# A fused attention and mixture-of-experts kernel: earlier q/k loads, spread setup steps, a fixed TensorE order in seven pairs, early first expert rows, and outputs issued behind weight conversions

## The chip, the core and the metric

The kernel runs on one core of a Trainium2 chip. A core has TensorE (called PE in the profile, its weight loads PEld), VectorE (DVE), ScalarE (ACT), GpSimd (POOL) and SyncE (SP, here a queue that issues DMAs). The metric is the device time of one execution in microseconds (us); lower is better.

## What is computed

First, causal attention over 8 batches and 8 heads with 576 positions and 64 channels, with a bias from a running sum of `max(s, 0)`. Its output is then the input of a routed network with 8 experts: each of the 4608 tokens takes the expert with the largest logit.

```python
scores = scale * np.matmul(q, k.transpose(0, 1, 3, 2))
cum = np.cumsum(np.maximum(s, 0.0), axis=-1)
bias = -(cum[:, :, :, None] - cum[:, :, None, :])
scores = np.where(causal, -1000000000.0, scores + np.minimum(bias, 0.0))
attn = softmax(scores)                     # written out in the reference
x = np.matmul(attn, v)                     # to (4608, 512)
logits = x @ w_gate + modality_bias[modality_id]
e_idx = np.argmax(logits, axis=1)
h = np.maximum(x[mask] @ w1[e], 0.0)       # for each expert e, its tokens
out[mask] = gate_w[mask, None] * (h @ w2[e])
```

## The kernel before, in words

**Attention** (`Attn`, lines 42 to 613). The work is cut into 32 *pairs*: one head of two batches. Eight pairs (the heads) make one of four *groups* of batches. A pair has nine score steps, in the order `ORDER = (3, 7, 2, 6, 8, 1, 5, 0, 4)`; the loop `run` (line 556) counts them with one counter `k`, so pair `k // 9`, position `k % 9`, 288 steps in all. A step does `score` (TensorE: a high product on line 374 and a low product on line 396, or lines 409 and 410 for step 8; DVE adds the mask and takes the maximum on line 398; ACT takes the exponential on line 421) and, three steps later (`LAG`), `trans`: TensorE transposes on line 441 into a PSUM tile `pt`, which ACT copies out on line 445. When a pair is through, `whole` multiplies by V (line 528), ACT copies `oT` (line 531), and line 348 projects into `x`, the network's rows. The last pair uses `tail` instead (lines 482 to 507).

q and k are split into a high and a low part for fp32r products: `prep` (line 314) makes them for the next pair on POOL, four high copies on line 324 and four differences on line 328. It needs the raw q and k of that pair (`load_qk`, line 306, issued by SP two pairs ahead, into two buffers each) and must not overwrite the `KA` buffer until the pair that still uses it is through its scores. `place` puts bias rows in by small DMAs (lines 264 and 283, six a pair in pairs 2 to 7; from pair 8 on two, lines 251 and 252, out of tables in DRAM that `save`, lines 189 and 191, writes in steps 21, 30, 39 and 48).

**What sets the order.** Instructions are traced in program order and a compile-time list scheduler orders each engine's queue by priority and by its own estimate of when operands are ready; at run time each queue is strictly in order. `issue_after(i)` adds an edge: what is traced within it comes behind `i` on `i`'s engine. `high_priority(offset)` raises priorities. `STRICT` (line 34) puts the transposes of steps 27 to 71 (pairs 3 to 7) behind the latest TensorE instruction of the attention; scores are free. `newest()` puts setup work behind the newest work of each engine. Setup functions run at given steps (dictionary `setup`, line 1414); a generator in `bg` goes on at every step when it yields `False`, at step n when it yields n.

**Routing** (`Route`). After each group, `group` computes logits, the one-hot expert, positions (ten small matmuls, line 775) and scatters the group's rows to per-expert lists in DRAM (line 799, nine scatters a group, 36 in all). After group 2, `first` builds the table `t2` of the first six blocks from groups 0 to 2 alone, which need the first 27 scatters. `pad` (line 817) writes 256 zero rows behind each of the eight lists. `rest` builds the tables `t3` and `t4`; their rows need all scatters and pads.

**Experts** (`Moe`, line 974). 18 blocks of 256 rows of one expert (6 of `t2`, 12 of `t3`), then a mixed block `two` and a loop for what is left. For a block, SP fetches rows (`gather2`, lines 1106 and 1107, into `xr` and `tg`) and `xt` (line 1113) makes them `xT`: two DVE transposes into PSUM (line 1120), a high copy on ACT (line 1122), a low difference on DVE (line 1123). The block's first half is 96 matmuls (line 1170, `hp`), evacuated as ReLU into high and low parts (lines 1172 and 1173); the second half is 48 matmuls (line 1145, `y`), evacuated with the gate by ACT (line 1155) and DVE (line 1153) into `ys`, which POOL scatters to the output (line 1156). The next block's `xt` is traced in the middle of a block (`mid`).

The weights of a block are eight *chunks* of 512 KB (four of w1, four of w2), loaded by SP (lines 1008 and 1010) into six raw buffers, and split into high (ACT, line 1033) and low (DVE, line 1034) in one of 13 converted buffers: 4 `wca`, 5 `wcb`, 4 `wcc`. Chunks 0 to 3 are converted by POOL (lines 1031 and 1034) while the attention ends (`early`, from step 278); the others come in steps of the blocks. `stop` limits how many chunks block 0 takes. The `wcc` buffers lie where the attention's rows `x` lay (pools `xp0` and `xp1`).

## Time and profile before

| | us |
|---|---|
| three runs | 810.08, 810.64, 811.33 (median 810.64) |
| profiled execution, device time | 811.94 |
| its span, first to last instruction | 810.2 |
| outside the span | 1.74 |
| mean granted TensorE clock | 0.988 |

How to read it: the page and the trace's views give times in us from the span's start. A timeline row is: start, duration, engine, line, operation, output tile <- input tiles, shapes, count, and in brackets the engine's idle time before it with what ended it. A row of the windows view is a stretch, its length, then for each engine the busy time and in brackets the number of instructions, the granted TensorE clock, the share of the 16 DMA engines and GB/s. "SPq" and "POOLq" are the engines' queues. Lines that several operations share are told apart by the tile names.

The attention lies from about 8 to 373 us, the expert blocks from 375 to 788 us, the rest to 810 us.

### The profile page before, as it was taken

To read this page: it belongs to the slowest core of one execution; us is meant where nothing else is said; L and a number is where in the kernel's file an instruction comes from. 1 tells how busy PE (TensorE), PEld (TensorE's weight loads), DVE (VectorE), ACT (ScalarE), POOL (GpSimd) and SP (SyncE) were. 2 spreads that over 40 slices of the span, in tenths; PEclk is the share of its full clock that TensorE was granted. 3 is DMA by queue.
4 is the path that set the end of the run, shared out by engine and by line. 5 is a ranking of instruction groups with operands and counts; after the bars stand their busy time and mean duration, and the time that the engine had idled before them with its cause. 6 is when DMAs were issued, how large, how long until landed. Compare 5 with 4: busy or idle time off the path is not lost. (4 is left out here: it accounts for less than half of the span.)

```text
span 810.2 us, 17263 instructions
## 1 busy us (share of the span) xinstructions
PE 790.2 (98%) x5796; PEld 684.1 (84%) x5796; DVE 565.5 (70%) x1441; ACT 519.6 (64%) x1165; POOL 363.9 (45%) x383
## 2 busy tenths in 40 slices
PE   8999999999999999998999999999999999999996
PEld 7787788888888888887888998888889998988884
DVE  7655667655766667767679786677777776677664
ACT  6877788878788778875455444555555555455553
POOL 8958877898789978993600100110000000001001
PEclk8999999999999999998999999999999999999999
DMA  7376644777567765659997897587878777877740
GB/s 238 116 214 195 220 147 155 258 235 230 158 183 240 229 186 175 213 160 292 300 319 240 282 291 256 174 273 228 255 252 263 249 247 240 261 256 259 257 170 29
DMA packets 88168, 181.21 MB, mean 224 GB/s; under 512 B 13785, under 2 KB 33113, under 8 KB 87950
## 3 DMA queue, kind: packets, MB, share of 16 engines
q1 hardware_dynamic: 82238, 160.03, 63.7%
q0 software_dynamic: 5840, 20.06, 6.3%
q8 instruction: 46, 0.75, 0.4%
q14 instruction: 44, 0.36, 0.1%
HBM read 143.59 MB, written 26.80 MB: 210 GB/s over the span
## 5 line engine op out<-in xcount | busy, mean ns | idle before, releaser
L1156 POOL DMA_INDIRECT out<-ys,oi x36 | 38.3, 1064 | 354.6 <-ACT ys L1155 274.8
L421 ACT ACTIVATE pe<-pe,mx 128x512 f32<-128x512 f32 (+3 forms) x256 | 142.3, 559 | 15.8 <-DVE mx L398 15.7
L398 DVE CUSTOM_DVE_ANT_0 pe<-sp,mk 128x512 f32<-128x512 f32 (+3 forms) x256 | 117.1, 482 | 49.1 <-PE sp L396 24.7
L445 ACT COPY PT<-pt 128x512 f32<-128x512 f32 (+1 forms) x192 | 94.2, 504 | 29.0 <-PE pt L441 28.9
L441 PE MATMUL pt<-ident,pe 128*128 128x128 f32 x640 | 106.4, 279 | 0.9 <-ACT PT L445 0.9
L374 PE MATMUL sp<-KA,QH 128*128 128x256 f32 (+2 forms) x256 | 97.4, 390 | 4.4 <-POOL KA L238 2.4
L1172 ACT ACTIVATE hT<-hp 128x512 fp32r<-128x512 f32 x72 | 43.1, 599 | 88.5 <-PE hp L1170 86.1
L1170 PE MATMUL hp<-xT,wca 128*128 128x256 f32 x624 | 88.6, 286 | 3.9 <-ACT xT L1122 2.5
L1170 PE MATMUL hp<-xT,wcb 128*128 128x256 f32 x648 | 90.1, 282 | 0.2 <-DVE wcb L1034 0.2
L328 POOL TENSOR_TENSOR QL<-rawq,QH 64x576 fp32r<-64x576 f32 x62 | 87.1, 1421 | 0.3
L328 POOL TENSOR_TENSOR KA<-rawk,KA 64x576 fp32r<-64x576 f32 x62 | 86.4, 1412 | 0.1
L1170 PEld LDWEIGHTS hp<-xT,wca 128*128 128x128 f32 x624 | 81.1, 194 | 5.5 <-issue 2.6
L396 PE MATMUL sp<-KB,QL 76*128 76x256 f32 (+2 forms) x256 | 84.5, 336 | 0.2 <-DMA QL<-ek 0.2
L441 PEld LDWEIGHTS pt<-ident,pe 128*128 128x128 f32 x640 | 77.4, 145 | 8.6 <-ACT PT L445 1.7
L528 PE MATMUL o<-PT,V 128*64 128x512 f32 (+1 forms) x496 | 84.5, 440 | 0.0
L1170 PEld LDWEIGHTS hp<-xT,wcb 128*128 128x128 f32 x648 | 83.3, 188 | 1.1 <-DVE wcb L1034 0.4
L1145 PE MATMUL y<-wcb,hT 128*128 128x512 f32 x336 | 80.9, 396 | 0.0
L1173 DVE SCALAR_TENSOR_TENSOR hT<-hp,hT 128x512 fp32r<-128x512 f32 x72 | 49.5, 688 | 42.7 <-ACT hT L1172 42.3
L1145 PEld LDWEIGHTS y<-wcb,hT 128*128 128x128 f32 x336 | 62.6, 188 | 14.5
L528 PEld LDWEIGHTS sp<-PT,V 128*64 128x64 f32 x620 | 38.2, 137 | 33.3 <-issue 28.5
L1170 PE MATMUL hp<-xT,wcc 128*128 128x256 f32 x456 | 64.3, 279 | 1.1 <-DVE hT L1173 0.7
L1145 PE MATMUL y<-wcc,hT 128*128 128x512 f32 x264 | 63.3, 395 | 0.0
(294 smaller groups left out, 1663.0 us busy)
## 6 DMA issues: line engine op xcount, KB each, us to landing
wrbw<-in_w SPq DMA_DIRECT2D x104, 512.0 KB
wraw<-in_w SPq DMA_DIRECT2D x56, 512.0 KB
rawq<-in_qkv SPq DMA_DIRECT2D x31, 576.0 KB
rawk<-in_qkv SPq DMA_DIRECT2D x31, 576.0 KB
V<-in_qkv SPq DMA_DIRECT2D x32, 320.0 KB
xr<-lists SPq DMA_DIRECT2D x72, 128.0 KB
KB<-KA SPq DMA_DIRECT2D x62, 144.0 KB
lists<-z SPq DMA_DIRECT2D x8, 576.0 KB
```

The lines of the kernel that those rows point to most:

```text
L328: self.last = nc.gpsimd.tensor_tensor(o, i, h, ALU.subtract).ins
L374: self.pe.append(self.nc.tensor.matmul(sp[:, :nn], QH[:, q0:q0 + P], self.KA[u][:, ab, :nn], start=True, stop=False).ins)
L396: self.pe.append(nc.tensor.matmul(sp[:, :nn], QL[:EXT, q0:q0 + P], KB[:EXT, ab, :nn], start=False, stop=True).ins)
L398: ins = nc.vector.tensor_tensor_reduce(out=t[:, :n], in0=sp[:, :n], in1=self.mk[:, 512 - n:512], scale=-0.125, scalar=3.0e38, op0=ALU.add, ...
L421: self.act = nc.scalar.activation(t[:, :n], t[:, :n], AF.Exp, bias=m, scale=-1.0, accum_out=st["sums"][:, o:o + 1]).ins
L441: self.pe.append(nc.tensor.transpose(out=pt[:, o:o + P], in_=pe[:, P * j:P * j + P], identity=self.ident).ins)
L445: return cp(w[:, :, :, v:v + P], pt[:, :n * (1 + both)].rearrange("p (a j q) -> p a j q", a=1 + both, q=P))
L528: m = nc.tensor.matmul(t[r, q0 - b:q1 - b], V[:, ab, j, :], PT[:, ab, PTS * j + q0 if j < 4 else PTW - 64:PTS * j + q1 if j < 4 else PTW], ...
L1145: self.last[0] = nc.tensor.matmul(y[u], hT[:, a, f, P * u:P * u + P], W[4 + f // 2][:, c, 512 * (f % 2):512 * (f % 2) + 512], start=f == 0 ...
L1170: nc.tensor.matmul(hp[:, u], W[k][:, a, f:f + P], xT[:, c, k], start=k == 0 and i == 0, stop=k == 3 and i == 2)
L1172: hi = nc.scalar.activation(hs, hp, AF.Relu)
L1173: lo = nc.vector.scalar_tensor_tensor(hT[:, 1, 2 * m:2 * m + 2], hp, 0.0, hs.bitcast(F32), ALU.max, ALU.subtract)
```

## The change

It does seven things. (1) `load_qk` is issued at position 4 of a pair, not 7. (2) The setup steps of the first pairs move: `R.consts` from step 14 to 15, `R.setup` from 20 to 24 with its five POOL parts at steps 33, 42, 51, 60 and 69, and `save` from steps 21, 30, 39, 48 to 25, 34, 43, 52, behind the load of their pair. (3) In steps 9 to 71 both scores and transposes come behind the latest TensorE instruction of the attention, so that TensorE's order there is the program's. (4) Block 0's rows are fetched from step 275 on as soon as 27 scatters are traced, into two buffers of the idle pool `xp0`; at step 288 DVE transposes them into SBUF and POOL makes the high part, and DVE the low part behind the last copies of the attention. `gather2` is split, so that `fetch_rows` holds its five DMAs. Block 0's gather, PSUM transposes and ACT copies are gone. (5) The weight conversions and the routing of the last group are then put behind the tail's last ACT copy and last DVE product (`fin`); the routing after its small matmuls has a lower priority (200 for 900). (6) Block 0 may take two more chunks, and `wcc` has four named buffers in a fixed order. (7) The two evacuations of block k into `ys` come behind the high and the low conversion of chunk 3 of block k + 1. The pads move from blocks 1 to 4 (two each) to blocks 2, 3 and 4 (two, three and three).

The diff, cut to its core (lines of the diff that are left out only pass arguments on or split `gather2`):

```diff
-STRICT = range(27, 72)
+STRICT = range(9, 72)
...
-        nc.scalar.copy(oT[:, q0:q0 + 256], o[:, :256])
+        self.fin = [nc.scalar.copy(oT[:, q0:q0 + 256], o[:, :256])]
...
-                nc.vector.tensor_copy(oT[r, 512 + 64 * ab:576 + 64 * ab], o[r, 256:320])
+                self.behind_x = nc.vector.tensor_copy(oT[r, 512 + 64 * ab:576 + 64 * ab], o[r, 256:320])
...
-        nc.vector.tensor_tensor(x[g][:, :, :, h], src.rearrange("p t (d r) -> p t d r", r=2), rv.rearrange("p t (d r) -> p t d r", r=2), ALU.mult)
+        self.fin.append(nc.vector.tensor_tensor(x[g][:, :, :, h], src.rearrange("p t (d r) -> p t d r", r=2), rv.rearrange("p t (d r) -> p t d r", r=2), ALU.mult))
         if g:
-            nc.vector.tensor_scalar(x[2][:, 0, :, h], xo[:, 4 * XW:5 * XW].rearrange("p (d r) -> p d r", r=2), rs[:, 8:9], None, ALU.mult)
+            self.behind_x = nc.vector.tensor_scalar(x[2][:, 0, :, h], xo[:, 4 * XW:5 * XW].rearrange("p (d r) -> p d r", r=2), rs[:, 8:9], None, ALU.mult)
...
+    def strict(self, k):
+
+        return self.tc.issue_after(self.pe[-1]) if self.pe and k in STRICT else ExitStack()
...
-                with self.behind() if pi or not self.pe else self.tc.issue_after(self.pe[-1]):
+                with self.behind() if pi or not self.pe else self.tc.issue_after(self.pe[-1]), self.strict(k):
                     exps = self.score(sts[pi], i)
...
-                if k % 9 == 7 and 0 < pi < npair - 2:
+                if k % 9 == 4 and 0 < pi < npair - 2:
                     self.raw[pi + 2] = self.load_qk(pi + 2)
...
-                with self.behind(), self.tc.issue_after(self.pe[-1]) if self.pe and k in STRICT else ExitStack():
+                with self.behind(), self.strict(k):
                     c = self.trans(sts[p0], i0)
...
+AHEAD = 3
 PRI2 = 900
+PRI3 = 200
...
+TURN = 288
...
-        for _ in range(20):
-            yield False
+        yield 33
         nc.gpsimd.tensor_copy(f, i)
         nc.gpsimd.tensor_copy(idf, ids.rearrange("p (t w) -> p t w", w=2)[:, :, 0])
-        yield False
+        yield 42
         for m in range(2):
             nc.gpsimd.tensor_scalar(sel[:, m], idf, float(m), None, ALU.is_equal)
-        yield False
         for m, d in ((0, self.mbs), (1, t0)):
+            yield 51 + 9 * m
             nc.gpsimd.tensor_tensor(d, sel[:, m].unsqueeze(2).broadcast_to([P, NT, 8]),
                                     mbb[:, 8 * m:8 * m + 8].unsqueeze(1).broadcast_to([P, NT, 8]), ALU.mult)
-            for _ in range(5):
-                yield False
+        yield 69
         nc.gpsimd.tensor_tensor(self.mbs, self.mbs, t0, ALU.add)
...
         of = ohb.rearrange("p t e -> p (t e)")
+        if not mm:
+            yield "mm"
         for u in range(10):
...
+        for n in ("ql", "hs"):
+            self.wc.tile([P, 512], F32, name=n, bufs=2)
+        for i in range(self.NC):
+            self.wc.tile([P, 2, 1024], F32R, name=f"wcc{i}")
...
-            w = self.wc.tile([P, 2, 1024], F32R, name="wcc", bufs=self.NC)
+            w = self.wc.tile([P, 2, 1024], F32R, name=f"wcc{(m - self.NB - self.NA + 2) % self.NC}")
...
-                nc.scalar.copy(w[:, 0], raw)
-            (nc.gpsimd if n in WGP else nc.vector).tensor_tensor(w[:, 1], raw, w[:, 0].bitcast(F32), ALU.subtract)
+                self.high = nc.scalar.copy(w[:, 0], raw).ins
+            self.conv.append((self.high, (nc.gpsimd if n in WGP else nc.vector).tensor_tensor(w[:, 1], raw, w[:, 0].bitcast(F32), ALU.subtract).ins))
...
-    def second(self, W, xg, oi, hT):
+    def second(self, W, xg, oi, hT, ahead):
...
-            if u:
-                self.last[1] = nc.vector.tensor_scalar(ys, y[u], gate, None, ALU.mult)
-            else:
-                self.last[3] = nc.scalar.activation(ys, y[u], AF.Copy, scale=gate)
+            with self.tc.issue_after(self.conv[ahead][u]):
+                if u:
+                    self.last[1] = nc.vector.tensor_scalar(ys, y[u], gate, None, ALU.mult)
+                else:
+                    self.last[3] = nc.scalar.activation(ys, y[u], AF.Copy, scale=gate)
...
+    def early_rows(self, pool, A):
+
+        nc, R = self.nc, self.R
+        while len(R.scat) < 27 or self.er is None:
+            yield False
+        a, b = (pool.tile([P, 4, XW // 2, 8, 2], F32, name="x").rearrange("p t d h r -> p (t d h r)") for _ in range(2))
+        tg, oi = R.c.tile([P, 2, 2], F32, name="tg0"), R.c.tile([P, 2], I32, name="oi0")
+        xr, xf = a[:, :1024].rearrange("p (t d) -> p t d", t=8), a[:, 1024:2048].rearrange("p (k n) -> p k n", k=4)
+        xT = b[:, :2048].bitcast(F32R).rearrange("p (a k n) -> p a k n", a=2, k=4)
+        self.fetch_rows(R.t2, self.er[1], xr, tg)
+        yield TURN
+        ks = [slice(0, 2), slice(2, 4)]
+        for k in ks:
+            A.hold[0] = nc.vector.transpose(out=xf[:, k].rearrange("p k (t n) -> p k t n", n=32),
+                                            in_=xr.rearrange("p t (d k) -> p k t d", k=4)[:, k]).ins
+            A.last = nc.gpsimd.tensor_scalar(xT[:, 0, k], xf[:, k], 1.0, 1.0, ALU.mult, ALU.mult).ins
+        for k in ks:
+            yield False
+            with self.tc.issue_after(A.behind_x.ins):
+                nc.vector.tensor_tensor(xT[:, 1, k], xf[:, k], xT[:, 0, k].bitcast(F32), ALU.subtract)
+        nc.vector.tensor_tensor(oi, tg[:, :, 1], R.t2["past"][:, 0], ALU.add)
+        self.first = ((None, tg), oi), xT
...
-            xg, oi = self.gather(tb, b, r, nu)
-            x = self.xt(xg, nu) if k == 0 else None
+            if early and k == 0:
+                (xg, oi), x = self.first
+            else:
+                xg, oi = self.gather(tb, b, r, nu)
+                x = self.xt(xg, nu) if k == 0 else None
...
             if early and k == 0:
-                self.stop = 8 + self.NB
+                self.stop = 8 + self.NB + 2
...
-                (self.two, self.quarter, self.block)[lst[k][2]](*cur, xT, mid)
+                (self.two, self.quarter, self.block)[lst[k][2]](*cur, xT, mid, *([8 * k + 8 + AHEAD] if lst[k][2] == 2 else []))
...
-            setup = {**A.more, 5: A.consts, 14: R.consts, 20: lambda: R.setup(mid, mb, A.t1p)}
+            setup = {**A.more, 5: A.consts, 15: R.consts, 24: lambda: R.setup(mid, mb, A.t1p)}
+            setup[275] = lambda: M.early_rows(xps[0], A)
             for p in range(4):
-                setup[21 + 9 * p] = lambda p=p: A.save(p // 2, p % 2)
+                setup[25 + 9 * p] = lambda p=p: A.save(p // 2, p % 2)
             bg = A.run(32, newx, done, setup)
+            M.tr = None, *A.fin
...
-                    for i in M.tr:
+                    for i in M.tr[1:]:
                         after.enter_context(tc.issue_after(i.ins))
-                    after.enter_context(tc.high_priority(offset=PRI2))
-                    for _ in bg[0][0]:
-                        pass
+                    with tc.high_priority(offset=PRI2):
+                        while next(bg[0][0]) != "mm":
+                            pass
+                    with tc.high_priority(offset=PRI3):
+                        for _ in bg[0][0]:
+                            pass
...
-                if 1 <= k <= 4:
+                if 2 <= k <= 4:
                     with tc.issue_after(M.hold), tc.issue_after(M.last[1].ins):
-                        R.pad((2 * k - 2, 2 * k - 1))
+                        R.pad(((0, 1), (2, 3, 4), (5, 6, 7))[k - 2])
```

More of the change, by code (lines that the diff above doesn't have):

```diff
@@ L983, in __init__ @@
         self.back = ()
+        self.er = None
+        self.conv, self.high = [], None
     def open(self, ctx):
@@ L1104, in gather2, with fetch_rows @@
         tg = self.mx.tile([P, 2, 2], F32, name="tg", bufs=3)
+        oi = self.mp.tile([P, 2], I32, name="oi", bufs=3)
+        self.fetch_rows(tb, r, xr, tg)
+        nc.vector.tensor_tensor(oi, tg[:, :, 1], tb["past"][:, bass.ds(b, 1), :].rearrange("p b u -> p (b u)"), ALU.add)
+        return (xr, tg), oi
+    def fetch_rows(self, tb, r, xr, tg):
+        nc = self.nc
         rows = self.R.lists[bass.ds(r, 2 * P), :]
@@ L1108, in gather2 @@
         self.rows(tb, i)
-        oi = self.mp.tile([P, 2], I32, name="oi", bufs=3)
-        nc.vector.tensor_tensor(oi, tg[:, :, 1], tb["past"][:, bass.ds(b, 1), :].rearrange("p b u -> p (b u)"), ALU.add)
-        return (xr, tg), oi
     def xt(self, xg, nu):
@@ L1158, in second, with block @@
                 in_=ys, in_offset=None, bounds_check=4607, oob_is_err=False)
-    def block(self, W, xg, oi, xT, mid):
+    def block(self, W, xg, oi, xT, mid, ahead):
         nc = self.nc
@@ L1177, in block @@
         mid()
-        self.second(W, xg, oi, hT)
+        self.second(W, xg, oi, hT, ahead)
     def quads(self, xg, k):
```

## The prediction

> **What bounds the kernel now.** I read the page first, then the windows over single pairs, the waits of TensorE, and then the timeline around each wait.
>
> ```profile
> span 810.2 us, 17263 instructions
> PE 790.2 (98%) x5796; PEld 684.1 (84%) x5796; DVE 565.5 (70%) x1441; ACT 519.6 (64%) x1165; POOL 363.9 (45%) x383
> ```
>
> TensorE is busy for 790.2 of 810.2 us, so the change cannot shorten a stage that is already full; it can only take away TensorE's 20 us of idle time and stretches in which it is slow. The two windows below hold the same work, four pairs with 386 matmuls each, one early and one late.
>
> ```profile
> core 0: us, PE busy (x) PEld busy (x) DVE busy (x) ACT busy (x) POOL busy (x), PEclk, DMA share, GB/s
> 53.55:101.51 47.96, 45.03 (x386) 36.03 (x380) 27.48 (x112) 35.15 (x105) 39.72 (x43) 1.00 0.69 214
> 156.05:199.30 43.25, 43.25 (x386) 36.48 (x380) 27.00 (x112) 34.73 (x104) 41.54 (x41) 1.00 0.74 231
> ```
>
> The late one is TensorE without a gap, 10.81 us a pair; the early one takes 47.96 − 43.25 = 4.7 us more. The waits name who is late:
>
> ```profile
> PE hp L1170 <- ACT xT L1122: 2.5, 1, 2.5
> ...
> PE sp L374 <- POOL KA L328: 1.7, 2, 1.2
> ...
> PE hp L1170 <- DVE wca L1034: 1.1, 3, 0.8
> PE pt L441 <- ACT PT L445: 0.9, 3, 0.3
> ```
>
> Three places follow: pairs 3 to 7 (POOL's KA and PT copies), the border between attention and experts (xT), and a few block starts (wca).
>
> **The change, part by part. A: pairs 1 to 7.**
>
> ```profile
> 26.38 0.88 PE L409 MATMUL sp<-KA,QH 128*128 128x288 f32 x2 [0.73 <-DVE mx L398]
> ...
> 58.02 0.85 PE L374 MATMUL sp<-KA,QH 128*128 128x512 f32 x3 [0.51 <-POOL KA L328]
> ...
> 70.47 0.85 PE L374 MATMUL sp<-KA,QH 128*128 128x512 f32 x3 [1.21 <-POOL KA L328]
> ...
> 73.73 0.65 PE L441 MATMUL pt<-ident,pe 128*128 128x128 f32 x4 [0.31 <-ACT PT L445]
> ```
> ```profile
> 39.26 1.17 SPq L311 DMA_DIRECT2D V<-in_qkv  x1
> ...
> 41.91 1.72 SPq L191 DMA_DIRECT2D eqd<-ek  x2
> 43.67 0.74 SPq L306 DMA_DIRECT2D rawq<-in_qkv  x1
> 44.45 0.44 SPq L306 DMA_DIRECT2D rawk<-in_qkv  x1
> ```
> ```profile
> 49.89 1.30 POOL L324 TENSOR_SCALAR KA<-rawk 128x576 fp32r<-128x576 f32 x2 [6.91 <-DMA rawk<-in_qkv]
> ...
> 55.18 2.79 POOL L328 TENSOR_TENSOR KA<-rawk,KA 64x576 fp32r<-64x576 f32 x2
> ...
> 81.92 0.79 POOL L730 TENSOR_TENSOR mbs<-mbs,mt 128x288 f32<-128x288 f32 x1
> ```
>
> TensorE wants pair 4's KA at 58.02 − 0.51 = 57.51 us. POOL needs 55.18 + 2.79 − 49.89 = 8.1 us for a pair's eight operations and began at 49.89, after idling 6.91 us for rawk, which SP issued at 44.45 (5.4 us to land). SP issued it late because setup DMAs and `save` stood between the V load (ended 40.43) and line 306 (43.67). With the load ahead of them, 43.67 − 40.43 = 3.2 us are gained: POOL ends near 54.8 and has 2.7 us to spare. Pair 5's wait, 1.21 us at 70.47, names the same line, and `save` stands ahead of its load too. The setup steps on POOL that fall into a pair are now one each, 0.79 us for the longest, inside that reserve. `save` and the two table loads move behind the raw load on SP; nothing needs their tables before pair 8 or the first routing, so I cost them nothing. If that cover were gone, the price would be their 3.2 us once.
>
> The rest of the 4.7 us is order: three high products stand ahead of their low products (the x3 in the rows at 58.02 and 70.47), and the transposes behind them then wait 0.31 us for a PT copy. With the program's order each high product is followed by its low one, as in the late window. The 0.73 us at 26.38 (pair 1, four high products holding all `sp` buffers) goes for the same reason. Ceiling: 4.7 + 0.73 = 5.4 us. The fixed order adds a wait, though: scores now queue behind transposes, and TensorE cannot slip past one that waits for ACT. No row shows that; The nearest row is line 441's wait for a PT copy in the list above: three times in the five pairs whose transposes were fixed already, each time behind three high products. So from below it costs 0 (nothing in it can gain beyond the ceiling), from above 0.31 us in each of seven pairs, 2.2 us. I take 0.2 in all, near the lower end, because the late window shows about the program's order and no gap. **A: −5.2 us (−3.2 to −5.4).**
>
> **B: the border.**
>
> ```profile
> 362.00:372.00 10.00, 9.43 (x90) 7.45 (x86) 4.97 (x21) 6.07 (x18) 7.44 (x5) 1.00 0.61 167
> ...
> 372.75:375.20 2.45, 0.00 (x0) 0.03 (x1) 2.41 (x5) 0.58 (x1) 0.00 (x0) 0.76 1.05 400
> 375.20:380.87 5.67, 5.67 (x26) 5.66 (x27) 5.53 (x11) 3.42 (x4) 0.00 (x0) 0.50 1.14 283
> ```
> ```profile
> 355.66 1.05 POOL L799 DMA_INDIRECT lists<-xq,di  x1 [0.17 <-ACT pe L421]
> ...
> 366.28 1.04 POOL L1031 TENSOR_SCALAR wca<-wraw 128x1024 fp32r<-128x1024 f32 x1
> ...
> 367.41 2.36 POOL L1034 TENSOR_TENSOR wca<-wraw,wca 128x1024 fp32r<-128x1024 f32 x1
> ...
> 373.16 1.08 DVE L1120 STREAM_TRANSPOSE tp<-xr 128x512 f32<-128x512 f32 x1
> ...
> 375.18 1.43 DVE L1123 TENSOR_TENSOR xT<-tp,xT 128x512 fp32r<-128x512 f32 x2
> ...
> 375.20 9.07 PE L1170 MATMUL hp<-xT,wca 128*128 128x256 f32 x54 [2.45 <-ACT xT L1122]
> ```
>
> TensorE stands still for 2.45 us, because the transposes start only at 373.16, and then has half the clock (0.50) for 5.67 us, which costs 5.67 × 0.5 = 2.84 us. The last of the 27 scatters is out at 355.66 + 1.05, so the rows can be fetched ten microseconds earlier than the transposes need them. In the window before the border DVE is busy 4.97 of 10 us: two transposes of 1.08 and two differences (1.43) fit, 3.6 us. POOL ends its last conversion at 367.41 + 2.36 = 369.77; its two high parts of half the width of line 1031 (1.04) take some 0.5 each, to 370.9. The differences are then through near 372.5, as the attention ends at 372.75. What is late next is the attention's tail itself: the transposes stand ahead of its small DVE copies, and delay them by 0 to 2.2 us; as DVE is half idle, I take 0.35. **B: −(2.45 + 2.84 − 0.35) = −4.9 us (0 to −5.3).**
>
> [...]
>
> Does block 0 keep the gain?
>
> ```profile
> 389.44 11.39 PE L1145 MATMUL y<-wcb,hT 128*128 128x512 f32 x48
> ...
> 391.08 1.07 ACT L1033 CAST wcb<-wrbw 128x1024 fp32r<-128x1024 f32 x1
> ```
>
> The weights of block 1 are converted from 391.08 on, just after TensorE left the first half (389.44) and its buffers came free. So they follow TensorE, and move ahead with it. The two more chunks of block 0, the routing's lower priority and the moved pads I cost at 0 (at worst 1 us): the lists that these feed are first read by block 6, and what covers the chunks is told under the rivals.
>
> **C: outputs behind weights.**
>
> ```profile
> 490.11 0.69 ACT L1155 ACTIVATE ys<-y,tg 128x512 f32<-128x512 f32 x1 [2.69 <-PE y L1145]
> 490.70 1.04 ACT L1033 CAST wcc<-wraw 128x1024 fp32r<-128x1024 f32 x1
> ...
> 514.01 0.69 ACT L1155 ACTIVATE ys<-y,tg 128x512 f32<-128x512 f32 x1 [4.85 <-PE y L1145]
> ...
> 516.48 1.04 ACT L1033 CAST wca<-wraw 128x1024 fp32r<-128x1024 f32 x1
> ...
> 538.64 0.69 ACT L1155 ACTIVATE ys<-y,tg 128x512 f32<-128x512 f32 x1 [1.98 <-PE y L1145]
> ...
> 561.23 0.69 ACT L1155 ACTIVATE ys<-y,tg 128x512 f32<-128x512 f32 x1 [3.02 <-PE y L1145]
> ```
>
> An undisturbed block takes 561.23 − 538.64 = 22.59 us; the two that begin near 490 and 514 take 23.90 and 24.63. At both starts ACT had idled (2.69 and 4.85 us) in front of the output copy, which waits for the block's end, with conversions queued behind it that the next block needs at once. The edge turns that round: three conversions of 1.04 fit into 4.85 us. The wait it adds holds up nothing: behind the outputs stand only chunks that the second half needs. **C: −(1.31 + 2.04) = −3.3 us (−2.0 to −3.4).**
>
> One such stall lies elsewhere and the edge does not reach it:
>
> ```profile
> 680.51 3.09 PE L1170 MATMUL hp<-xT,wcc 128*128 128x256 f32 x24 [0.71 <-DVE hT L1173]
> ```
>
> It is an accident of the queue's order. The change re-orders every queue, so I add one new accident of this size, rounded to +1.0 (0 to +3).
>
> **Sum.** −5.2 − 4.9 − 3.3 + 1.0 = −12.4 us. The profiled execution took 811.94 us (span 810.2 and 1.74 around it) and would take 799.5; it lies 1.3 above the median of the runs, 810.64, from which I get 798.2.
>
> **The rivals.** *The border stays.* If the early xT comes late (POOL's high parts behind its conversions, DVE held by a fetch), the gap stays, and the clock falls again; B is 0 and the time 803.1. For it: POOL is busy to 369.77. Against: from there to 372.75 are 3 us, for 1 us of POOL's work and 0.7 us of the last difference. *Transfers become the bound.* DMA share is 1.14 at the border, and TensorE comes 5 us earlier with two more chunks asked for; if block 1's weights land no sooner, B is given back: also 803. Against: conversions waited for buffers there. *The fixed order costs more than it frees.* If transposing steps wait 0.31 us each, 49 of them in seven pairs lose 15.2 us; against the other parts' 12.4 that gives 813.4, slower. It decides from 40 waiting steps on. Against: the late window shows nearly this order without a gap. *The change does not do what it says at the block starts.* If ACT idled at 490 and 514 because the raw chunks had not landed, the edge moves nothing forward and only puts the output copies behind a late DMA; C is 0 and the time 798.2 + 3.3 = 801.5. For it: nothing in ACT's rows says why it idled. Against it stands the issue of the chunk that was converted at 516.48:
>
> ```profile
> 496.43 0.33 SPq L1008 DMA_DIRECT2D wraw<-in_w  x1
> ```
>
> That is 20 us ahead, nearly four times what rawk took to land.
>
> **How the numbers follow.** Forecast 0.60; border 0.15; transfers 0.09; block starts 0.10; fixed order costs 0.06. The first four are all faster by more than 0.2% (1.6 us, about what a measurement of this kernel can tell), save a corner in which several fail together (0.04). So faster 0.90, same 0.04, slower 0.06. The range reaches from the ceilings (−5.4 − 5.3 − 3.4 = −14.1, with a lucky order 795.0) to the border rivals with A at its low end and a second accident, 803.1 + 2.0 + 1.0 = 806.1.
>
> **What would show it.** Right: four pairs from pair 3 on in 43.3 us, no wait of line 374 for KA; no gap and clock 1.00 at the border, block 0 within 22.7 us; the blocks near 490 and 514 at 22.6, their chunk-3 conversions ahead of the output copy. Wrong: a row of TensorE at line 1170 that waits for xT or a new POOL row at the border; waits of 0.3 us at line 441 in every early pair; block 1 waiting for its weights.

## The result, and the profile after

| | runs | median us | range us |
|---|---|---|---|
| before | 4 | 810.36 | 809.98 to 811.33 |
| after | 4 | 803.83 | 803.34 to 804.30 |

The ratio is 0.9918 (95% interval 0.9900 to 0.9935): 6.5 us faster. The direction held and the time lies in the stated range, but the forecast was 798.2: the change gave about half of the 12.4 us that were summed. The profiled execution took 804.30 us (span 802.6) against 811.94 (810.2).

From the page of the kernel after, the span and the busy times:

```profile
span 802.6 us, 17274 instructions
PE 787.1 (98%) x5796; PEld 682.7 (85%) x5796; DVE 568.0 (71%) x1441; ACT 518.5 (65%) x1163; POOL 364.3 (45%) x385
```

TensorE is still busy 98% of the span. Its idle time fell from 20.0 to 15.5 us, and its busy time by 3.1 us. Time at half clock counts as busy (in the kernel after, 3.41 of the 3.41 us from 16.85 on, at a granted clock of 0.50), and the clock was halved for 10.2 us at the start of the execution before (12.23 to 22.47) and for 3.4 us at the start of this one (16.85 to 20.26).

**Pairs 3 to 6**, with pairs counted from 0 (windows view; the stretch goes from the end of pair 2 to the end of pair 6, an end being the copy of `oT` on line 531, and has the same 386 matmuls as the one shown for before):

```profile
52.33:96.87 44.54, 43.97 (x386) 35.99 (x380) 26.93 (x112) 35.05 (x104) 34.87 (x40) 1.00 0.69 219
```

44.54 us instead of 47.96; the late window had 43.25. The list of TensorE's waits has no entry for KA of line 328 any more. What it has instead is a short wait for ACT's copy of PT in three pairs, and, new, the border:

```profile
PE ox L348 <- DVE oT L489: 1.7, 1, 1.7
...
PE ox L348 <- DVE xq L507: 0.8, 1, 0.8
PE pt L441 <- ACT pe L421: 0.8, 3, 0.3
...
PE pt L441 <- ACT PT L445: 0.6, 3, 0.2
```

**The border.** The wait of 2.45 us for xT is gone, and the first expert product (line 1189 after, 1170 before) follows the attention without a gap. But two waits stand in the attention's own tail now. TensorE's timeline:

```profile
367.28 0.44 PE L348 MATMUL ox<-pq,oT 128*128 128x72 f32 x2 [1.73 <-DVE oT L489]
...
369.36 1.30 PE L348 MATMUL ox<-pw,oT 128*128 128x144 f32 x4 [0.84 <-DVE xq L507]
370.29 1.01 PE L1189 MATMUL hp<-x,wca 128*128 128x256 f32 x3
```

The reason is in the rows of VectorE, and beside them GpSimd's, both in the kernel after:

```profile
363.67 1.16 DVE L1370 STREAM_TRANSPOSE x<-x 128x512 f32<-128x512 f32 x1
364.69 0.23 DVE L495 RECIPROCAL rs<-rs 128x9 f32<-128x9 f32 x1
364.78 2.08 DVE L1377 TENSOR_TENSOR oi<-tg,no 128x2 int32<-128x2 f32 x1
366.78 0.45 DVE L489 COPY oT<-o 64x64 f32<-64x64 f32 x2
367.46 1.08 DVE L1376 TENSOR_TENSOR x<-x 128x512 fp32r<-128x512 f32 x1 [0.23 <-POOL x L1372]
368.56 0.46 DVE L505 TENSOR_TENSOR x<-ox,rs 128x288 f32<-128x288 f32 x1
368.93 0.28 DVE L507 TENSOR_SCALAR xq<-ox,rs 128x72 f32<-128x72 f32 x1
```
```profile
364.50 2.34 POOL L1047 TENSOR_TENSOR wca<-wraw,wca 128x1024 fp32r<-128x1024 f32 x1
366.81 1.20 POOL L1372 TENSOR_SCALAR x<-x 128x512 fp32r<-128x512 f32 x2
```

`oi`, an index of 128 x 2 numbers, takes 2.08 us; it ends at 366.86, as GpSimd's low part of a weight chunk ends (364.50 + 2.34 = 366.84). Behind it in the queue stands oT's copy of line 489, for which TensorE waits. Then the first low part of xT waits for GpSimd's high part, and lines 505 and 507 stand behind it. With these waits the clock falls as before (windows of the kernel after; the number behind POOL's is the granted clock):

```profile
365.00:368.42 3.42, 1.69 (x14) 1.12 (x13) 3.17 (x4) 0.10 (x1) 3.01 (x3) 1.00 1.04 393
368.42:371.83 3.41, 2.57 (x13) 2.50 (x12) 2.44 (x7) 0.37 (x1) 0.00 (x0) 0.50 1.24 241
371.83:375.24 3.41, 3.41 (x18) 3.41 (x18) 2.22 (x11) 1.47 (x3) 0.00 (x0) 0.50 0.63 237
```

So, if the clock is counted as in the prediction, the border cost 0.47 + 2.45 us of waits (the 0.47 was in the tail already) and 5.67 × 0.5 = 2.84 by the clock before, 5.76 in all; after, 1.73 + 0.84 and (2.57 + 3.41) × 0.5 = 2.99, 5.56. The account of B below shows that this counts the clock too high, before and after. From the last oT copy of line 531 to the first expert product it takes 12.84 us after, 12.76 before.

**The blocks.** ScalarE's rows around the two block starts that had been slow:

```profile
483.47 1.05 ACT L1046 CAST wcc<-wraw 128x1024 fp32r<-128x1024 f32 x1
484.42 1.05 ACT L1046 CAST wcb<-wrbw 128x1024 fp32r<-128x1024 f32 x1
486.40 0.69 ACT L1174 ACTIVATE ys<-y,tg 128x512 f32<-128x512 f32 x1 [0.93 <-PE y L1163]
...
505.51 1.99 ACT L1046 CAST wca<-wrbw 128x1024 fp32r<-128x1024 f32 x2
507.40 1.05 ACT L1046 CAST wca<-wraw 128x1024 fp32r<-128x1024 f32 x1
509.02 0.69 ACT L1174 ACTIVATE ys<-y,tg 128x512 f32<-128x512 f32 x1 [0.57 <-PE y L1163]
...
531.09 0.69 ACT L1174 ACTIVATE ys<-y,tg 128x512 f32<-128x512 f32 x1 [1.98 <-PE y L1163]
```

The conversions now stand ahead of the output copies, and ScalarE idles 0.93 and 0.57 us there instead of 2.69 and 4.85. From copy to copy it is 22.62 and 22.07 us; before 23.90 and 24.63.

### The profile page after: what moved, and what is told of

Its sections match the earlier page's. It is cut to its first block, busy times and chain, and to the rows that moved or that the text cites. A ratio compares the mean times of both kernels' runs of the same rounds, so it can differ in the third digit from the quotient of the medians.

```text
span 802.6 us, 17274 instructions
## 1 busy us (share of the span) xinstructions
PE 787.1 (98%) x5796; PEld 682.7 (85%) x5796; DVE 568.0 (71%) x1441; ACT 518.5 (65%) x1163; POOL 364.3 (45%) x385
## 5 line engine op out<-in xcount | busy, mean ns | idle before, releaser
L421 ACT ACTIVATE pe<-pe,mx 128x512 f32<-128x512 f32 (+3 forms) x256 | 142.4, 559 | 12.5 <-DVE mx L398 12.4
L1189 PE MATMUL hp<-xT,wca 128*128 128x256 f32 x528 | 73.4, 279 | 0.0
L1189 PEld LDWEIGHTS hp<-xT,wca 128*128 128x128 f32 x528 | 66.9, 188 | 0.5
```

Source lines behind the costliest of these rows:

```text
L421: self.act = nc.scalar.activation(t[:, :n], t[:, :n], AF.Exp, bias=m, scale=-1.0, accum_out=st["sums"][:, o:o + 1]).ins
L1189: nc.tensor.matmul(hp[:, u], W[k][:, a, f:f + P], xT[:, c, k], start=k == 0 and i == 0, stop=k == 3 and i == 2)
```

## The experiments

Ratios are to the kernel before on the same chip in the same set of runs: 810.01 us for A alone, C alone and the two runs with a changed index, 810.62 for order alone, loads alone, A and C without B and the high parts on ScalarE, 809.75 for the others.

### The parts alone

**A alone**: the kernel before with

```diff
-STRICT = range(27, 72)
+STRICT = range(9, 72)
-                with self.behind() if pi or not self.pe else self.tc.issue_after(self.pe[-1]):
+                with self.behind() if pi or not self.pe else self.tc.issue_after(self.pe[-1]), self.strict(k):
-                if k % 9 == 7 and 0 < pi < npair - 2:
+                if k % 9 == 4 and 0 < pi < npair - 2:
```

and the moved setup steps.

> The kernel before with part A alone: loads of q and k at position 4, setup steps spread, fixed order in pairs 1 to 7; border and outputs as before. If A is worth what the comparison of the two traces says (5.0 us at the end of pair 29, of which 3.0 lie at the start and may be the phase of the halved clock, not the order): 805.6 with the early clock as after, 808.6 with the early clock as before. My prediction's value for A was 5.2 (805.4). Pairs 3 to 6 should take 44.5 us, pair 1 to pair 2 12.8 instead of 11.1 in either case.

Measured: 806.50 us, ratio 0.9960 (0.9944 to 0.9975), 3.5 us faster. The expectations count pairs from 1 where they say "from pair 1 to pair 2": they mean the time from the first oT copy of line 531 to the second, which end pairs 0 and 1 here. It was 12.36 us, expected 12.8. **Order alone** has the first two edits, **loads alone** the third and the setup steps:

> The kernel before with TensorE's fixed order in pairs 1 to 7 alone; loads and setup steps where they were. By the prediction's sum the order is worth 4.7 - 0.51 - 1.21 + 0.73 - 0.2 = 3.5 us (806.5 from 810.0), with the two waits of line 374 for KA still there near 58 and 70. Rival: the order pays only with the early loads, since a fixed TensorE cannot slip past a score that waits for KA; then it is 809 to 811 and the waits of line 374 are longer than 0.51 and 1.21.

> The kernel before with the loads of q and k at position 4 and the setup steps spread, TensorE's order as before. By the prediction's sum the two waits for KA go, 0.51 + 1.21 = 1.7 us, so 808.3. Rival (the early loads are what makes the order of the high and low products come out well): all of part A, 805.5 to 806.5. Pair 1 to pair 2 should be near 11.1 to 12 if the fixed order is what makes that pair wait, 12.4 or more if the moved setup steps are.

Order alone: 807.56, ratio 0.9962 (0.9948 to 0.9975), −3.1. Loads alone: 809.09, ratio 0.9983 (0.9970 to 0.9995), −1.5; its rival, all of part A, fell. From the first oT copy to the second it took 11.04 and 10.97 us: neither part alone makes that stretch longer than the 11.11 before. The four pairs from pair 3 on in A alone, in order alone and in loads alone (windows):

```profile
52.47:96.96 44.49, 43.98 (x386) 35.96 (x380) 26.94 (x112) 35.06 (x105) 34.89 (x40) 1.00 0.68 219
```
```profile
52.23:98.43 46.20, 44.58 (x386) 36.50 (x380) 27.39 (x112) 35.40 (x104) 38.48 (x42) 1.00 0.71 219
```
```profile
52.08:99.39 47.31, 45.02 (x386) 35.96 (x380) 27.43 (x112) 35.18 (x105) 38.42 (x42) 1.00 0.71 222
```

Against 47.96 that is −1.76 for the order and −0.65 for the loads, and −3.47 for both. That is more than the sum, 2.41, but in C alone, whose code here is the kernel before's, the same stretch took 47.02, so single executions do not settle it; in the runs' medians both together (−3.5) gave less than the sum (−4.6), within the intervals. What the rows do show is that each alone leaves the other's wait in place. First order alone, then loads alone, TensorE in pair 4 to 5:

```profile
68.00 0.50 PE L374 MATMUL sp<-KA,QH 128*128 128x512 f32 x1 [0.69 <-POOL KA L328]
...
69.72 0.50 PE L374 MATMUL sp<-KA,QH 128*128 128x512 f32 x1 [0.55 <-POOL KA L328]
```
```profile
67.24 0.80 PE L374 MATMUL sp<-KA,QH 128*128 128x512 f32 x3
68.39 0.44 PE L374 MATMUL sp<-KA,QH 128*128 128x384 f32 x1 [0.35 <-DVE mx L398]
```

With the order alone TensorE takes high and low in turn, but POOL's KA is late. With the loads alone KA is there, and TensorE again takes three high products in a row and stands before the fourth. The rival for the order, that it pays only with the loads (809 to 811), fell.

**C alone**: the kernel before with the two edges

```diff
+                self.high = nc.scalar.copy(w[:, 0], raw).ins
+            self.conv.append((self.high, (... tensor_tensor(...)).ins))
...
+            with self.tc.issue_after(self.conv[ahead][u]):
                 if u:
```

> The kernel before with part C alone: each block's output copies behind the conversions of the chunk three ahead. Prediction: 3.3 us (807.3 from 810.6), the blocks that took 23.90 and 24.63 at 22.6. The traces before and after differ by 3.9 us over those three blocks, so 806.5 if the edge alone does that. Rival (the other edits that differ there, the chunk tiles by name and the earlier stop count, do it): no gain, 810.6.

Measured: 806.67, ratio 0.9961 (0.9945 to 0.9977), 3.3 us faster, as predicted; the two blocks took 22.56 and 22.07 us, where A alone still has 23.89 and 24.63. The rival fell.

**A and C without B**: both sets of edits, the border as before.

> The kernel before with parts A and C together, the border as before. If B is worth nothing net, as the two traces say (12.76 us before, 12.84 after, from line 531's last copy to the first expert product): 803.5 to 804, like the kernel after. If B gives what I predicted and something else took it back: 804 + 4.9 = 808 to 809. If B costs time net: 802 to 803.

Measured: 802.77 us (802.34 to 803.34), ratio 0.9905 (0.9888 to 0.9923). The kernel after, with B, has 803.83 (803.34 to 804.30). So B gives nothing: by the ratios (0.9918 − 0.9905 = 0.0013) it loses 1.1 us, and with both half-widths of 0.00175 taken together (0.0025) that lies between −1 and +3 us. B is here all that A and C leave out, so also the two more chunks of block 0, the order of the `wcc` buffers, the routing's lower priority and the moved pads. In the two profiles the border is about the same (38.69 us with B and 38.52 without, from the last oT copy to block 1's first product), and what lies behind it, to the end of the span, takes 406.5 us with B and 405.4 without. So in these profiles the loss lies in the blocks; which of those other edits makes it, no run tried.

### What stopped B

**The index from one input**, in the same place. tg is added to 0 instead of to `past`, which is zero for this block:

```diff
-        nc.vector.tensor_tensor(oi, tg[:, :, 1], R.t2["past"][:, 0], ALU.add)
+        nc.vector.tensor_scalar(oi, tg[:, :, 1], 0.0, None, ALU.add)
```

> The kernel after, with the index oi of the first block made from one tile of SBUF instead of two (tg plus the constant 0 instead of tg plus past, which is zero for this block). Place and order on VectorE stay. Theory (the two inputs hold the operation until GpSimd's low part of a weight chunk is through): the operation takes about 0.15 us instead of 2.08, oT's copy behind it moves up by some 1.5 us, the wait of 1.73 us that TensorE has in front of line 348 at 365.56 shrinks below 0.5; the time is 799.5 to 802.3 (803.8 minus 1.5 without and 4.3 with the half clock gone). Rival (its place or a semaphore holds it, not the two inputs): it still takes about 2 us, the wait stays at 1.7 and the time at 803.8.

**The same index with two inputs, later**:

```diff
-        nc.vector.tensor_tensor(oi, tg[:, :, 1], R.t2["past"][:, 0], ALU.add)
+        with self.tc.issue_after(A.behind_x.ins):
+            nc.vector.tensor_tensor(oi, tg[:, :, 1], R.t2["past"][:, 0], ALU.add)
```

> The kernel after, with the same two-input operation oi, traced behind the attention's last small product x (line 507), when GpSimd has finished its chunk. Theory of the two inputs: about 0.15 us there, as GpSimd reads nothing then or is in a one-input operation; the wait in front of line 348 falls below 0.5 us, time 799.5 to 802.3 as with one input. If it is held there as well (about 1 to 2 us) then GpSimd's one-input high parts block it too, and the low parts behind it come later: 803 to 805. Rival (oi waits for its fetched row tg to land, whatever its inputs): the wait in front of line 348 goes away too, but the one-input kernel keeps its 2 us.

Measured: 804.40 (ratio 0.9930, 0.9914 to 0.9946) and 803.55 (0.9925, 0.9908 to 0.9941): no gain, against the theory's time. But the operation did what the theory said, in both. VectorE with one input, then TensorE of that kernel, then VectorE with two inputs, later:

```profile
365.50 0.17 DVE L1377 TENSOR_SCALAR oi<-tg 128x2 int32<-128x2 f32 x1
365.57 0.45 DVE L489 COPY oT<-o 64x64 f32<-64x64 f32 x2
368.70 1.08 DVE L1376 TENSOR_TENSOR x<-x 128x512 fp32r<-128x512 f32 x1 [2.68 <-POOL x L1372]
369.79 0.46 DVE L505 TENSOR_TENSOR x<-ox,rs 128x288 f32<-128x288 f32 x1
```
```profile
370.60 1.11 PE L348 MATMUL ox<-pw,oT 128*128 128x144 f32 x4 [3.28 <-DVE xq L507]
```
```profile
370.24 0.15 DVE L1378 TENSOR_TENSOR oi<-tg,no 128x2 int32<-128x2 f32 x1
```

`oi` takes 0.17 and 0.15 us, and the wait for line 489 is gone. The first low part (line 1376) then reaches the head of VectorE's queue sooner and waits 2.68 us for GpSimd's high part, with lines 505 and 507 behind it, so TensorE waits 3.28 us once instead of 1.73 + 0.84. What the theory missed is the second operation in the same queue.

In the run with one input, GpSimd's two-input operation happened to start only behind `oi` (at 365.73), so that run doesn't tell the number of inputs from the meeting. In the kernel after a reciprocal and a transpose, with one input each, ran 0.23 and 1.16 us beside the GpSimd operation that held `oi`. But one input is not enough to go free. In C alone the routing constant `ew`, made from one tile of 128 x 8, stands among the scores of pair 2, here with GpSimd's copies:

```profile
33.00 2.93 DVE L686 TENSOR_SCALAR ew<-e 128x8 f32<-128x8 f32 x1
```
```profile
33.28 1.30 POOL L324 TENSOR_SCALAR KA<-rawk 128x576 fp32r<-128x576 f32 x2
34.56 1.30 POOL L324 TENSOR_SCALAR QH<-rawq 128x576 fp32r<-128x576 f32 x2
```

It took 2.93 us and ended at 35.93, as the fourth of these copies did (35.86), and TensorE behind it waited 1.09 us for line 398; in order alone the same operation took 0.16 us, and in the kernel after 0.16 us too, at 33.92, beside the first two copies there (33.32 to 34.63). So which VectorE operations GpSimd holds is not told by the number of inputs alone, and these runs leave it open.

**Low parts and index behind the tail**, the high parts still on GpSimd:

```diff
-        for k in ks:
-            yield False
-            with self.tc.issue_after(A.behind_x.ins):
-                nc.vector.tensor_tensor(xT[:, 1, k], ...)
-        nc.vector.tensor_tensor(oi, tg[:, :, 1], R.t2["past"][:, 0], ALU.add)
+        yield False
+        yield False
+        with self.tc.issue_after(A.behind_x.ins):
+            for k in ks:
+                nc.vector.tensor_tensor(xT[:, 1, k], ...)
+            nc.vector.tensor_tensor(oi, tg[:, :, 1], R.t2["past"][:, 0], ALU.add)
```

> The kernel after with only VectorE's order at the border changed: both low parts of xT and the two-input index oi stand behind the attention's last small product x (line 507); the high parts stay on GpSimd. Theory (VectorE's queue held the tail, and GpSimd's late high parts hold the experts): TensorE's waits in the tail fall to about 0.5 us each as in the kernel before, but the high parts still end near 369, so a wait of 1 to 2 us comes up in front of the first expert product: 802 to 803. Rival (the order on VectorE was all): no wait there, 800.4 as with the high parts on ScalarE.

Two steps later, `behind_x` names line 507; in the kernel after it still named the copy of line 489 when the first low part was traced. Measured: 801.15 us (801.08 to 801.26), ratio 0.9879 (0.9852 to 0.9906). VectorE, then TensorE:

```profile
366.71 0.28 DVE L507 TENSOR_SCALAR xq<-ox,rs 128x72 f32<-128x72 f32 x1
368.38 1.69 DVE L1377 TENSOR_TENSOR x<-x 128x512 fp32r<-128x512 f32 x2 [1.39 <-POOL x L1372]
```
```profile
369.52 5.68 PE L1189 MATMUL hp<-x,wca 128*128 128x256 f32 x46 [0.61 <-DVE x L1377]
```

The tail is undisturbed; VectorE still waits 1.39 us for GpSimd, but with nothing of the tail behind it. TensorE starts the experts with the high parts at 368.40 and then waits 0.61 us for a low one: less than the 1 to 2 us expected.

**The same with the high parts on ScalarE** (and one input for `oi`, again 0 in place of past's zeros):

```diff
-            A.last = nc.gpsimd.tensor_scalar(xT[:, 0, k], xf[:, k], 1.0, 1.0, ALU.mult, ALU.mult).ins
+        yield False
+        yield False
+        for k in ks:
+            A.act = nc.scalar.copy(xT[:, 0, k], xf[:, k]).ins
```

> The kernel after with the border mended: the two transposes at the same place, the two high parts of xT on ScalarE instead of GpSimd, and both low parts and the index oi (one input; tg plus 0, as past is zero for this block) behind the attention's last small product x (line 507). Theory (VectorE, queued in order, held the attention's last small copies for GpSimd's work, and that is all that B lost): no wait above 0.5 us in front of line 348, first expert product near 367.7 instead of 370.3, no half clock there unless the remaining gap fills over half of a 3.4-us stretch; time 803.8 - 2.6 = 801.2, with the clock's 3.4 as well 797.8. Rival (the border is bound elsewhere, by the raw weights of the first chunks or by the transposes' place): a new wait of 2 us at the first expert products, and 803 to 804.

Measured: 800.43 us (800.23 to 802.66), ratio 0.9887 (0.9866 to 0.9908), span 798.5: the fastest of all by its median, 3.4 us under the kernel after (2.5 by the ratios). This is the mended border in what follows. Its last waits, on TensorE:

```profile
365.82 0.76 PE L348 MATMUL ox<-pw,oT 128*128 128x144 f32 x4 [1.07 <-ACT oT L485]
...
368.03 0.76 PE L348 MATMUL ox<-pw,oT 128*128 128x144 f32 x4 [0.47 <-ACT oT L485]
368.53 7.71 PE L1189 MATMUL hp<-x,wca 128*128 128x256 f32 x61
```

The clock stays at 1.00 here, with TensorE busy for 2.34 and 2.94 us of the two stretches of 3.41 us in which these waits lie (363.39 to 370.21). The border's waits are 1.07 + 0.47 = 1.54 us. From the last oT copy to block 1's first product it takes 34.96 us instead of 38.69, 3.7 less, of the 802.6 − 798.5 = 4.1 by which the spans differ. With the low parts behind the tail alone it is 35.77, so 2.9 of the 3.7 us come from VectorE's order and 0.8 from the high parts' engine and the index.

### Three details on top of the mended border

```diff
-            setup = {**A.more, 5: A.consts, 15: R.consts, 24: lambda: R.setup(mid, mb, A.t1p)}
+            setup = {**A.more, 5: A.consts, 14: R.consts, 24: lambda: R.setup(mid, mb, A.t1p)}
```

> The kernel with the mended border (high parts on ScalarE, low parts and oi, one input with 0 for past's zeros, behind the tail), and the routing's constants back at step 14, where they stood before, instead of 15. Theory (the moved constants, on VectorE among pair 2's first scores, make the fixed order wait): from pair 1 to pair 2 it takes 11.0 us instead of 12.2 to 12.8, and the time falls from 800.4 to 799.2. Rival (the fixed order alone makes pair 2 wait): 12.2 and 800.4 as before this edit; the run with the order alone, where the constants stood at 14 and the pair took 11.04, speaks against it.

```diff
-STRICT = range(9, 72)
+STRICT = range(27, 72)
```

> The kernel with the mended border, TensorE's order fixed only from pair 3 on (steps 27 to 71) for scores and transposes, the constants at step 15. If it is the fixed order in pairs 1 and 2 together with the moved constants that costs, pair 1 to pair 2 takes about 11 us and the time is 799.2, as with the constants at 14; the wait of 0.73 us for mx near 25 comes back and takes 0.7 of it: 799.9. Rival (the constants' place alone costs, whatever the order): 12.2 again and 801.

Measured: 801.29 (799.95 to 807.61) and 801.48 (799.78 to 802.89); neither differs from 800.43 beyond their scatter. The times at which the first two pairs end (the oT copies of line 531, one execution each):

| kernel | end of pair 0 | end of pair 1 | between |
|---|---|---|---|
| before | 31.62 | 42.73 | 11.11 |
| order alone | 30.29 | 41.33 | 11.04 |
| loads alone | 30.28 | 41.25 | 10.97 |
| A alone | 29.20 | 41.56 | 12.36 |
| after | 28.65 | 41.42 | 12.77 |
| mended border | 29.17 | 41.32 | 12.15 |
| mended, constants at 14 | 29.45 | 41.02 | 11.57 |
| mended, order from 27 | 31.85 | 42.82 | 10.97 |
| C alone | 29.91 | 43.52 | 13.61 |

For 12.15 us the two runs expected about 11 and took 11.57 and 10.97, but the table does not bear out that the fixed order and the moved constants are the cause, and the times that were expected, 799.2 and 799.9, did not come. The fixed order alone costs nothing here, nor do the early loads with the moved steps; C alone, with neither, takes longest, with `ew` held as shown above. Kernels that left pair 0 between 28.6 and 30.3 left pair 1 between 41.0 and 41.6, C alone excepted: what A gains ahead of this stretch is lost in it. Why, and what that is worth in time, stays open.

The third has the constants at 14 as well:

```diff
-TURN = 288
+TURN = 287
```

> As with the mended border and the constants at 14, the transposes and high parts one step sooner (287). Theory: the wait of 1.07 us that the tail still has in front of line 348 (ScalarE's second high part stands ahead of oT's copy) goes, so 0.5 to 1.0 us less than without this edit: 798.4. Rival: one step sooner the rows have not landed or the transposes hold the last score's copies, and it is 799.2 or more.

Measured: 806.03 us (803.12 to 809.13), 4.7 more than with the constants at 14 alone, and not for the rival's reason. The transposes hardly moved (362.49 us), and the wait that was to go was still 1.04 us; the low parts, traced one step sooner, came ahead of line 507 again, on VectorE:

```profile
366.06 1.73 DVE L1378 TENSOR_TENSOR x<-x 128x512 fp32r<-128x512 f32 x2
...
368.46 0.28 DVE L507 TENSOR_SCALAR xq<-ox,rs 128x72 f32<-128x72 f32 x1
```

TensorE waited 1.57 us for line 507, and the clock fell. This repeats B's fault. The trace accounts for 3.3 us of it (span 801.5 against 798.2); why the other runs of this kernel were up to 6 us longer than the profiled one is open.

## Why the prediction was right in direction and about twice too large

**C** (−3.3 predicted, −3.3 alone, interval −1.9 to −4.5). Right in mechanism and size: conversions ahead of the output copy, block lengths of 22.6 and 22.1. The rival that the raw chunks land late fell.

**A** (−5.2 predicted, −3.5 alone, interval −2.0 to −4.5). Right in mechanism: the KA waits go with the loads, the x3 order with the edge. Two terms were too large. The 4.7 us of the four pairs were 3.5: they were to come down to 43.25 us and came to 44.5, with TensorE busy 43.98 and a wait of about 0.2 us for PT in three pairs; and part of the 4.7 was chance of one execution, as C alone took 47.02 there and not 47.96 with the same code. Why TensorE was busy 0.7 us longer than in the late window is not shown. And the 0.73 us of pair 1 did not last: A alone ends pair 0 1.1 us sooner than order alone or loads alone, and pair 1 no sooner than they do, with two waits of 0.3 us at line 441 for ACT's exponential that before did not have. The 0.2 us for the fixed order is not shown to be at fault, as order alone took 11.04 us there.

A comparison of the two profiles alone would have given A 5.0 us, with 3.0 of them before pair 0 ends. Much of that is chance: C alone, whose code there is the kernel before's, had one stretch of half clock at the start instead of three, was 1.7 us sooner at the end of pair 0 (29.91 against 31.62), lost it in pair 1, and at the end of pair 6 was at 101.36 against 101.51.

**B** (−4.9 predicted, +1.1 measured, −1 to +3). This is the step that failed: "What is late next is the attention's tail itself: the transposes stand ahead of its small DVE copies, and delay them by 0 to 2.2 us; as DVE is half idle, I take 0.35." The question was right, the size wrong. The tail lost 1.73 + 0.84 − 0.47 = 2.10 us, and the clock fell again for it, 2.99 us by the prediction's count. It wasn't the transposes, which stand in the same place in the run with the low parts behind the tail, where neither wait is left: it was `oi`, which the sum had not priced as an instruction at all, and a low part that waits for GpSimd. Half idle on average says nothing of a queue in strict order: the low part that waited 2.68 us in the run with one input for `oi` held lines 505 and 507 behind it, and TensorE waited 3.28 us. The rival "the border stays" is what happened, though in the tail and not at line 1170; that its 803.1 lies so near is in part luck, since it still had A at −5.2 and a new accident in it.

Two more terms of B were off. The clock's 2.84 us was too large. Block 0, from its first product to block 1's, takes 25.47 us before, with 5.67 us of it at half clock; at full clock it takes 24.31 in C alone and 23.95 with the mended border. So the full clock is worth 1.2 to 1.5 us there, about half of what was summed, and the whole border, once mended, gave 38.23 − 34.96 = 3.3 us, not 4.9. And the edits that the sum put at 0 (at worst 1 us) are what is left for the 1.1 us that the blocks take longer than in A and C without B.

In the rows `oi` took 2.08 us beside GpSimd's two-input operation (line 1047, 2.34 us), and 0.15 us at 370.24 in the run that has it later, where GpSimd had ended its work of the border at 368.51. The prediction took 1.43 us for the two low parts, as line 1123 had needed; they took 1.08 and 0.68 us, and the cost lay in what stood behind `oi`.

**The accident** (+1.0). No new one came; the old one stayed, in the kernel after's TensorE rows:

```profile
673.32 0.87 PE L1189 MATMUL hp<-xT,wcc 128*128 128x256 f32 x5 [0.69 <-DVE hT L1192]
```

The sum as measured: A and C alone make −6.8, together −7.9 (their intervals allow both), and with B −6.5. The range's lower end, 795.0, lies 1.5 us below 810.64 − 14.1 = 796.5; no row prices the "lucky order" that it stands for.

## What to carry to other kernels

When work is moved under the end of another stage, list every instruction that it puts into each in-order queue, the smallest too, and ask of each what it waits for and who stands behind it; the mean load of the engine doesn't answer that. Place moved work behind the last instruction that the critical engine waits for, and on the engine that then has nothing late in its queue. When one wait is removed and the time stays, look at the next instruction in the same queue before dropping the theory.

## What the runs showed of the hardware

**Half clock came in stretches of 3.41 us.** Wherever the clock was halved at the border, it was for 3.41 or 6.83 us; at the start for 10.24 before and for 3.41 after: multiples of 3.413. Within an execution the changes lie whole numbers of such stretches apart (before, 12.23 to 374.04 is 106 of them; after, 16.85 to 368.42 is 103), and they fall differently in each (a stretch begins at 370.63 before and at 370.19 in C alone). The same gap of 2.45 us at the border (waits of 0.47 and 2.45) was followed by half the clock before and not in C alone. First before, then C alone, each cut at these stretches:

```profile
370.63:374.04 3.41, 1.65 (x13) 1.03 (x12) 1.91 (x4) 0.37 (x1) 0.00 (x0) 1.00 1.01 379
374.04:377.45 3.41, 2.25 (x10) 2.26 (x11) 3.30 (x8) 2.73 (x4) 0.00 (x0) 0.50 1.12 308
377.45:380.87 3.42, 3.42 (x18) 3.42 (x18) 3.38 (x6) 1.27 (x2) 0.00 (x0) 0.50 1.13 293
```
```profile
370.19:373.60 3.41, 1.91 (x16) 1.23 (x14) 1.65 (x4) 0.37 (x1) 0.00 (x0) 1.00 0.96 337
373.60:377.01 3.41, 1.88 (x13) 1.70 (x14) 3.30 (x7) 2.47 (x4) 0.00 (x0) 1.00 1.10 339
```

Where TensorE was busy 1.65 of 3.41 us the next stretch had half the clock; where the gap fell across a boundary, leaving 1.91 and 1.88, it had 1.00. In the other kernels, all stretches at the border with 1.74 us or less (1.74 in the last run above) were followed by half the clock, none with 1.88 or more: idle time of 1.67 us, less than half a stretch, was enough, where the expectation for the mended border had over half. At half clock, stretches with 2.25 to 2.83 us busy were followed by another slow one, those with 3.29 or more by full speed. So with the border's code as before, the clock was not halved in C alone, and it was halved for 3.41 us in order alone and loads alone and for 6.83 before. What that cost was less than half of the time: block 0 took 24.31 us in C alone and 25.47 before, where 5.67 us of it had half the clock.

**A very small operation took nearly as long as another engine's beside it.** 128 x 2 numbers (`oi`) took 2.08 us on VectorE beside a GpSimd operation of 2.34 us, and 0.15 to 0.17 in the two runs where it did not meet that operation; where it did, it ended within 0.02 us of GpSimd's end. 128 x 8 numbers (`ew`) took 2.93 us beside four GpSimd copies in C alone, and 0.16 beside the first two in the kernel after.
